# Attention, a token and channel mixer and a Fourier layer on one core: separate PSUM tiles for the banks of scores, transposes and the first stage, one exponential per block of queries, another table of the planner

## The chip, the cores and the metric

The kernel runs as one program on one core of a Trainium2 chip. The metric is the device time of an execution in microseconds (us). Before the change the median of 3 runs is 1688.03 us (1684.77 to 1692.13). One further execution was profiled; its own time is 1692.11 us.

TensorE (PE) multiplies matrices and writes only to PSUM, a memory of eight banks of 128 partitions by 512 words. VectorE (DVE) and ScalarE (ACT) read PSUM and write the results to SBUF, GpSimd (POOL) works in SBUF alone, and SyncE (SP) starts the DMAs. Each engine works off its own instructions in the order in which the program gives them, and waits at an instruction for semaphores that other engines raise.

## The reference

Attention over 4 batches of 8 heads, with 576 queries (neighbouring pairs of 1152 rows are averaged) and 1152 keys of 64 numbers; then two layers on the 4 x 576 x 512 result:

```python
q_pool = q.reshape(B, H, S // 2, 2, D).mean(axis=3)
scores = scale * np.matmul(q_pool, k.transpose(0, 1, 3, 2))
scores = scores - np.max(scores, axis=-1, keepdims=True)
attn = np.exp(scores)
attn = attn / (np.sum(attn, axis=-1, keepdims=True) + 1e-09)
x = np.matmul(attn, v)                               # heads side by side: 4 x 576 x 512

h = np.maximum(xt @ w_tok1, 0.0) @ w_tok2            # xt: tokens last; 576 -> 256 -> 576
u = x + h.transpose(0, 2, 1)
x = u + np.maximum(u @ w_ch1, 0.0) @ w_ch2           # 512 -> 1536 -> 512

u = x + np.real(np.fft.fft(np.fft.fft(x, axis=1), axis=2))
un = (u - mu) / np.sqrt(var + 1e-06)                 # over the 512 channels
out = u + np.maximum(un @ w_ch1, 0.0) @ w_ch2        # 512 -> 2048 -> 512
```

All of it is float32 with float64 weights for the mixers.

## The kernel before

Most products are made of several float32r products, of a number's rounded part ("hi") and its rest ("lo"): ACT copies a PSUM tile rounded, DVE subtracts that copy from the tile.

**Three stages.** (1) Heads 0 to 7 (`ALONE = 8`; functions `first_peaks`, `first_unit`) find the maxima first and make the scores with keys on the partitions. Their PSUM tiles are two pairs of banks (ring `pss_r`): PE writes the scores of two key blocks (line L742), ACT takes the exponential (L747), PE multiplies by the values (L754). (2) Heads 8 to 31 (`peaks`, `unit`, five blocks of 128 queries a head, the last of 66): PE writes a block's scores into three banks in six products of 384 columns (L637), DVE finds the row's maximum over the three banks (`nm<-m`, L644), ACT takes the exponential into SBUF with the sum beside it (`s<-m,nm`, L649) in two instructions, one over two banks and one over the third. Later PE turns `s` over, 128 x 128 at a time (L793), into a PSUM bank, ACT copies that rounded (`ph`, L797), DVE makes the rest (`pl`, L800), and PE multiplies both by the values into the tile `av` (L807). Beside these heads runs the mixer of the batch before (`mix`, L914 to L1038, weights converted from float64 on ACT, POOL and DVE in `slot`), whose products fill PE between the steps of attention. (3) The last batch's mixer, the Fourier layer (L1155, L1174) and the last channel mixer (L1442, L1501).

**PSUM.** One bank is `av`, three are the pool of `bank` tiles, which the mixer, the transposes and others share, and four are one tile, `m`:

```python
m_tile = ps_s.tile([128, 4, 512], F32, name="m", bufs=1)
pss_r = Ring(2, two, True)                                   # stage 1: m_tile[:, 0:2], m_tile[:, 2:4]
m3_r = Ring(3, lambda: m_tile[:, next(turn_3) % 3])          # stage 2: scores
t_bank = Ring(1, lambda: m_tile[:, 3])                       # stage 2: every second group of transposes
ps, ph, pl = Buf(t_bank if gr % 2 else banks), Buf(ph_r), Buf(pl_r)
```

So in stage 2 a head's groups of transposes go in turn to a `bank` tile and to the fourth bank of `m`; the trace shows them as `bank<-ident,s` and `m<-ident,s`.

**Order.** Nothing is ordered while the kernel runs. Every operation is given to a planner (`Plan`) with an engine, an estimated cost, a due time and its predecessors; the due time is shifted by a number from the table `SHIFT`. The planner runs a list schedule over the engines (`order`): whenever an engine is free, it takes the ready operation with the earliest due time whose ring has room. The order of taking is the order in which the program is written, and each engine keeps it. Semaphores are put in afterwards by the layer below, from the tiles that instructions read and write, and not from the planner's predecessors.

Of the kernel before, what the change touches and what calls it, by code (L numbers as in the profile page):

```python
# [10 lines left out]
F32 = mybir.dt.float32  # L11
# [20 lines left out]
PB = 5  # L32
# [29 lines left out]
    "cvld": 18.13, "cabs": 224.94, "cclamp": 670.62, "cshift": 760.61, "csign": 337.54, "cexp": 234.92, "cword":  # L62
    67.48, "cmul": 295.11, "cadd": 413.34, "chi": 147.28, "csub": 412.44, "cvst": 12.96, "cs": -377.28, "warm.":
    302.33, "l.": -504.19, "q.": -172.47, "qh.": 261.8, "ql.": -251.03, "kh.": 149.84, "kl.": 33.1, "M.":
    -589.13, "mr.": -66.27, "zh.": -31.41, "mr2.": -564.09, "zl.": -842.44, "mT.": 113.74, "mrow.": -729.51,
    "vld": -190.88, "S.": -511.53, "exp.": 571.95, "AV.": -220.28, "xe.": 223.11, "turn": -12.73, "rs": 1.74,
# [6 lines left out]
    "AV": -0.01, "xe": 0.2, "xa": -231.39, "open": -26.94, "sqrt": -563.36, "fcld": -177.35, "fchi": -19.77,  # L73
    "fclo": 939.3, "nyld": -271.24, "nyh": -694.66, "fld": 11.96, "FPUT": 293.06, "DFT": -6.81, "Zh": 398.17,
    "Zl": 102.01, "PB": -31.35, "PA": -31.32, "bs": -552.84, "pm": -30.79, "yadd": -115.75, "u2st": 433.32,
    "dwld": 8.26, "dwv": 9.66, "dwh": -444.21, "dwl": -424.67, "mixover": 120.41, "fnetover": -188.88, "uld":
    -353.69, "bn": 99.88, "bnr": -116.71, "un": -351.91, "dturn": -126.93, "dth": 21.37, "dtl": -264.84, "L":
    129.06, "drl": -119.51, "dll": -135.45, "dadd": 425.75, "dst": 485.52, "TB": -658.08, "TH": 528.64, "TL":
    -1176.01, "TA": 254.23, "WR": 157.96, "WH": -43.89, "WL": -140.73, "VR": -598.67, "LP": -688.42, "LE":
    1013.96, "LC": -997.5, "LH": -14.88, "LL": 318.59, "LQ": 872.8,  # L80
# [32 lines left out]
class Op:  # L113
    def __init__(self, key, eng, cost, due, emit, deps, after, new, uses):
        self.key = key
        self.moves = eng in ("SP", "AQ")
        eng = "A" if eng == "AQ" else eng
        self.eng, self.cost, self.due, self.emit, self.new, self.uses = eng, cost, due, emit, new, uses
# [10 lines left out]

def lag(a, b):  # L130
    if a == b:
        return 0.13 if a == "V" else 0.0
    return 0.26 if b == "T" else 0.2


class Plan:
# [14 lines left out]
    def order(self):  # L151
# [10 lines left out]
        while len(out) < len(self.ops):  # L162
# [8 lines left out]
            for eng, q in ready.items():  # L171
# [21 lines left out]
                busy = best.end  # L193
# [7 lines left out]
                heapq.heappush(wait, (best.end + 0.2, -1))  # L201
# [8 lines left out]
    def room(self, ring, now):  # L210
        return len(ring.live) < ring.n or all(u.end is not None and u.end + 0.2 <= now for u in ring.live[0].users)
# [9 lines left out]
def tile_attention_moe_fnet(  # L221
# [51 lines left out]
    with tc.manual_schedule():  # L273
# [12 lines left out]
        ps_s = pool("ps_s", space=PSUM, side="right")  # L286
# [22 lines left out]
        def t_dma(n):  # L309
            return n / 235e3  # L310
# [25 lines left out]
        def conv64(due, src, outs, parts, sums=None):  # L336
# [17 lines left out]
            a = add("cabs", "A", t_act(n), due, lambda: nc.scalar.activation(out=f32(hi()), in_=words(F32, 1), func=AF.Abs),  # L354
                    [o], uses=[w])
            a = add("cclamp", "P", t_pool(n), due, lambda: nc.gpsimd.tensor_scalar(  # L356
# [10 lines left out]
            o = add("cword", "A", t_act(n), due, lambda: nc.scalar.activation(  # L367
# [99 lines left out]
        def two():  # L467
            i = 2 * (next(turn_2) % 2)
            return m_tile[:, i:i + 2]
# [30 lines left out]
        def totals(i):  # L500
            t = sp.tile([128, 5, 2], F32, name=f"sum{i}", bufs=1)
# [14 lines left out]
        def first_pair():  # L516
            for g in range(2):
                x, kk, k2, qq = Buf(x_r[g]), Buf(kk_r), Buf(k2_r), Buf(qq_r)
                due = 30 * g - 40
                q_parts = ((0, 256), (256, NQ)) if g == 0 else ((0, NQ),)  # L520
# [58 lines left out]
        def pair(p):  # L579
# [3 lines left out]
            lq = add("lq", "SP", t_dma(128 * 8 * NQ), due, lambda: nc.sync.dma_start(  # L583
                out=f32(qx.t), in_=qT[b, h:h + 2].rearrange("h d t n -> (h d) t n")), new=[qx])
            lk = add("lk", "SP", t_dma(128 * 4 * S), due, lambda: nc.sync.dma_start(
# [3 lines left out]
            q = add("qs", "P", t_pool(NQ), due + 0.5, lambda: nc.gpsimd.tensor_scalar(  # L589
# [1104 lines left out]
```

## Time and profile before

| | |
|---|---|
| median of 3 runs | 1688.03 us |
| profiled execution | 1692.11 us, span 1690.3 us (first to last instruction) |
| PE busy | 1486.4 us, 88% of the span, 9019 products |
| DVE, ACT, POOL busy | 988.1 us (58%), 807.5 us (48%), 566.8 us (34%) |
| granted TensorE clock, mean | 0.95 of full |
| DMA | 270.37 MB, 160 GB/s mean |

A row of the page's costliest groups gives line, engine, operation, tile written, tile read, shape and count, then busy time and mean duration, then the time for which that engine sat idle just before these instructions and what ended it. In the page's slices PE is 7 to 9 tenths busy up to two thirds of the span and 9 tenths or more from there. The first score product of stage 2 starts at 189.0 us, the last transpose at 1135.6 us.

### The profile page before, as it was taken

The page shows a single profiled execution, that of the slowest core. Times are in us where ns is not written, and L with a number is a line of the kernel's source. Part 1 is how long each engine was busy: PE and PEld are TensorE (multiplying, and loading weights), DVE is VectorE, ACT ScalarE, POOL GpSimd, SP SyncE. Part 2 cuts the span into 40 slices and gives each one's busy share as a digit, 9 for nine tenths or more (in the row PEclk, how much of TensorE's full clock was granted, in tenths as well). Part 3 has the DMA queues.
Part 4 walks back from the last instruction along what each step waited for, and adds up shares of the span by engine and source line. Part 5 has one row for each costly group of instructions (what it writes and reads, how often), then busy time and mean ns, then how long its engine had stood idle before and what let it go on. Part 6 is the DMA issues. An engine that isn't in the chain of part 4 may idle for free.

```text
span 1690.3 us, 24731 instructions
## 1 busy us (share of the span) xinstructions
PE 1486.4 (88%) x9019; PEld 1320.4 (78%) x9019; DVE 988.1 (58%) x1854; ACT 807.5 (48%) x1774; POOL 566.8 (34%) x468
## 2 busy tenths in 40 slices
PE   8999887889787878878878877889999999999999
PEld 6677676778676767777757777788998988999997
DVE  7665555656665545566654656555766575647542
ACT  4445566555555555554555555444223354425331
POOL 4667844444354524254544444310111000000000
PEclk8999899988998879999998999989999999999999
DMA  5767665454555535455655454217762655454352
GB/s 144 208 176 199 205 175 148 138 174 122 169 160 161 157 94 158 132 161 162 187 150 160 139 176 140 90 60 228 240 188 73 220 187 174 159 203 162 141 185 93
DMA packets 112179, 270.37 MB, mean 160 GB/s; under 512 B 9971, under 2 KB 37748, under 8 KB 111767
## 3 DMA queue, kind: packets, MB, share of 16 engines
q1 hardware_dynamic: 112058, 268.79, 52.6%
q8 instruction: 71, 1.16, 0.3%
q14 instruction: 50, 0.41, 0.1%
HBM read 191.15 MB, written 44.86 MB: 140 GB/s over the span
## 4 chain that ended last, share of the span: by engine, by line
PE 51%; ACT 9%; DVE 8%; issue 3%; DMA 1%; POOL 0%; ACTq 0%; SPq 0%; DVEq 0%; POOLq 0%
PE bank L1442 8%; PE bank L999 7%; PE m L637 7%; PE y L1501 6%; ACT s L649 5%; DVE nm L644 5%; PE bank L979 4%; PE c L1501 4%; PE m L793 3%; ACT ph L797 3%; DVE pl L800 2%; PE bank L1312 2%; PE y L1334 2%; PE av L807 2%; PE c L1155 1%
## 5 line engine op out<-in xcount | busy, mean ns | idle before, releaser
L637 PE MATMUL m<-kk,qq 128*128 128x384 f32 (+1 forms) x720 | 188.8, 383 | 85.4 <-ACT s L649 61.0
L649 ACT ACTIVATE s<-m,nm 128x768 f32<-128x768 f32 (+1 forms) x240 | 177.0, 739 | 106.1 <-DVE pl L800 38.9
L644 DVE TENSOR_REDUCE nm<-m 128x1 f32<-128x1152 f32 (+1 forms) x120 | 162.5, 1354 | 98.6 <-PE m L793 40.5
L637 PEld LDWEIGHTS m<-kk,qq 128*128 128x128 f32 (+1 forms) x720 | 120.0, 192 | 126.0 <-ACT s L649 84.1
L979 PE MATMUL bank<-ut,w 128*128 128x320 f32 (+1 forms) x1152 | 190.6, 312 | 6.5 <-DVE pl L800 4.2
L800 DVE TENSOR_TENSOR pl<-m,ph 128x512 fp32r<-128x512 f32 (+1 forms) x144 | 80.1, 556 | 185.2 <-ACT s L649 70.1
L979 PEld LDWEIGHTS bank<-ut,w 128*128 128x128 f32 x1152 | 171.9, 202 | 8.9 <-issue 5.1
L999 PE MATMUL bank<-h,w 128*128 128x320 f32 (+1 forms) x1152 | 163.3, 298 | 1.6 <-DVE pl L800 1.0
L999 PEld LDWEIGHTS bank<-h,w 128*128 128x128 f32 x1152 | 157.6, 191 | 3.1 <-DVE pl L800 1.4
L1442 PE MATMUL bank<-tt,wc 128*128 128x320 f32 x1008 | 157.1, 309 | 1.2 <-DVE e L1456 1.1
L1442 PEld LDWEIGHTS bank<-tt,wc 128*128 128x128 f32 x1008 | 151.9, 188 | 6.6 <-DVE e L1456 1.3
L356 POOL TENSOR_SCALAR slot<-slot 128x512 f32<-128x512 f32 (+2 forms) x62 | 117.5, 1899 | 117.6 <-ACT slot L354 107.7
L797 ACT ACTIVATE ph<-m 128x512 fp32r<-128x512 f32 (+1 forms) x144 | 70.6, 490 | 176.0 <-DVE nm L644 78.6
L793 PE MATMUL m<-ident,s 128*128 128x128 f32 (+1 forms) x480 | 84.7, 296 | 72.3 <-ACT s L649 36.1
L807 PE MATMUL av<-ph,vv 128*128 128x256 f32 (+1 forms) x432 | 141.7, 343 | 2.0 <-DVE xtr L819 1.5
L369 POOL TENSOR_TENSOR slot<-slot 128x512 f32<-128x512 f32 (+2 forms) x62 | 81.3, 1312 | 175.9 <-DVE slot L364 151.5
L807 PE MATMUL av<-pl,vv 128*128 128x256 f32 (+1 forms) x432 | 129.5, 315 | 8.7 <-DVE pl L800 8.7
L793 PEld LDWEIGHTS m<-ident,s 128*128 128x128 f32 (+1 forms) x480 | 60.8, 155 | 94.5 <-ACT s L649 44.7
L797 ACT ACTIVATE ph<-bank 128x512 fp32r<-128x512 f32 (+1 forms) x192 | 88.8, 468 | 86.9 <-PE bank L793 84.7
L800 DVE TENSOR_TENSOR pl<-bank,ph 128x512 fp32r<-128x512 f32 (+1 forms) x192 | 99.1, 524 | 19.6 <-ACT ph L797 19.0
L1501 PE MATMUL y<-v,hp 128*128 128x512 f32 x432 | 108.2, 392 | 0.0
L1008 DVE TENSOR_TENSOR yt<-bank,yt 128x256 f32<-128x256 f32 (+1 forms) x192 | 85.4, 453 | 28.7 <-PE bank L999 26.2
(163 smaller groups left out, 2950.3 us busy)
## 6 DMA issues: line engine op xcount, KB each, us to landing
w<-wb_d SPq DMA_DIRECT2D x96, 512.0 KB
slot<-in_wm_dram SPq DMA_DIRECT2D x56, 512.0 KB
v<-w_d SPq DMA_DIRECT2D x24, 1024.0 KB
raw<-w_d SPq DMA_DIRECT2D x24, 896.0 KB
kk<-kx SPq DMA_DIRECT2D x66, 288.0 KB
wb_d<-slot SPq DMA_DIRECT2D x24, 512.0 KB
v<-in_v_dram SPq DMA_DIRECT2D x32, 292.5 KB
qx<-in_qT_dram SPq DMA_DIRECT2D x15, 576.0 KB
```

The source lines that it names most:

```text
L356: a = add("cclamp", "P", t_pool(n), due, lambda: nc.gpsimd.tensor_scalar(out=f32(hi()), in0=f32(hi()), scalar1=F64_LO, scalar2=F64_HI, op0 ...
L637: nc.tensor.matmul(m.t[:n, :KW], qq.t[:r, t, q0:q0 + n], kk.t[:r, c * KW:(c + 1) * KW], start=(t == 0), stop=(t == 1))
L644: a = add("mx" + own_place, "V", t_dve(S), d + 0.05, lambda n=n, j=j: nc.vector.tensor_reduce(out=nm.t[:n, j:j + 1], in_=m_tile[:n, :3, :K ...
L649: done.append(add("exp" + own_place, "A", t_act(KW * (c1 - c0)), d + 0.1, lambda s=s, n=n, j=j, k=k, c0=c0, c1=c1: nc.scalar.activation(ou ...
L793: nc.tensor.transpose(ps.t[:, at:at + r], made[j][0].t[:r, c * 128:(c + 1) * 128], ident[:r, :r])
L797: a = add("hi", "A", t_act(n), due + 0.1, lambda ps=ps, ph=ph, n=n: nc.scalar.activation(out=ph.t[:, :n], in_=ps.t[:, :n], func=AF.Copy), ...
L800: b = add("lo", "V", t_dve(n), due + 0.2, lambda ps=ps, ph=ph, pl=pl, n=n: nc.vector.tensor_tensor(out=pl.t[:, :n], in0=ps.t[:, :n], in1=f ...
L807: nc.tensor.matmul(po.t[:, :nq], vv.t[:, c].rearrange("p s d -> p (s d)"), x.t[:, k * nq:(k + 1) * nq], start=c == 0 and x is ph, stop=c = ...
L979: mms.append(lambda ps, k=len(mms), kk=kk, wi=wi, xi=xi, t0=t0, n=n: nc.tensor.matmul(ps[:, :n], view("p (s k n) -> p s k n", s=2, k=4)[:, ...
L999: mms.append(lambda ps, k=len(mms), x=x, wi=wi, hi=hi, cc=cc, t0=t0, n=n: nc.tensor.matmul(ps[:, :n], ww[x][2]("p (s n) -> p s n", s=2)[:, ...
L1442: nc.tensor.matmul(ps.t[:, :PH], w.t[:, wi, k, 128 * kk:128 * kk + 128], x.t[:, xi, kk], start=(first and m == 0), stop=(last and m == 5), ...
L1501: nc.tensor.matmul(y.t, h.t[:, k, hi, j * 128:(j + 1) * 128], v.t[:, wi, k], start=(q == 0 and k == 0 and n == 0), stop=(q == 7 and k == 1 ...
```

## The change

Four parts. (a) `m` is taken apart. Stage 1 has a pool of two tiles `s` of two banks. When the exponentials of head 7 are planned, that pool is closed, and in its place two tiles are opened: `m` of three banks for scores and `tr` of one bank for every second group of transposes. (b) The two exponentials of a block become one over 1152 columns, its sum is one number instead of two, and the DVE instruction that added the two goes. (c) The planner's costs change (hand-over times, an overlap of successive instructions on one engine, DMA rates, a least cost on DVE), and so do all numbers of `SHIFT`. (d) The operation that ends stage 1 waits for its exponentials alone.

```diff
 SHIFT = {
-    "cvld": 18.13, "cabs": 224.94, "cclamp": 670.62, "cshift": 760.61, "csign": 337.54, "cexp": 234.92, "cword":
+    "cvld": 76.82, "cabs": 1780.99, "cclamp": 658.29, "cshift": 534.18, "csign": 159.7, "cexp": 523.06, "cword":
...
+OVERLAP = {"A": 0.1, "V": 0.083, "P": 0.04}
+
+
 def lag(a, b):
-    if a == b:
-        return 0.13 if a == "V" else 0.0
-    return 0.26 if b == "T" else 0.2
+    if b == "T":
+        return 0.0 if a == "T" else 0.16 if a in OVERLAP else 0.26
+    if a == "T" or a not in OVERLAP or b not in OVERLAP:
+        return 0.2
+    if a == b == "A":
+        return -0.1
+    return 0.08 if b == "P" else 0.035
...
-                busy = best.end
+                busy = best.end - OVERLAP.get(eng, 0.0)
...
-            return n / 235e3
+            return n / 390e3
...
-        m_tile = ps_s.tile([128, 4, 512], F32, name="m", bufs=1)
-        turn_2 = iter(range(10 * ALONE))
+        m_tile = []
...
-        pss_r = Ring(2, two, True)
-        m3_r = Ring(3, lambda: m_tile[:, next(turn_3) % 3])
-        t_bank = Ring(1, lambda: m_tile[:, 3])
+        pss_r = Ring(2, lambda: early_s["s"].tile([128, 2, 512], F32, tag="s", name="s", bufs=2), True)
+        m3_r = Ring(3, lambda: m_tile[0][:, next(turn_3) % 3])
+        t_bank = Ring(1, lambda: m_tile[1])
...
-                done = []
-                for k, (c0, c1) in enumerate(((0, 2), (2, 3))):
-                    done.append(add("exp" + own_place, "A", t_act(KW * (c1 - c0)), d + 0.1, lambda s=s, n=n, j=j, k=k, c0=c0, c1=c1: nc.scalar.activation(
-                        out=s.t[:n, KW * c0:KW * c1].rearrange("p (c n) -> p c n", n=KW), in_=m_tile[:n, c0:c1, :KW], func=AF.Exp,
-                        bias=nm.t[:n, j:j + 1], accum_out=total.t[:n, j, k:k + 1]), [a],
...
+                o = add("exp" + own_place, "A", t_act(S) + 0.18, d + 0.1, lambda s=s, n=n, j=j: nc.scalar.activation(
+                    out=s.t[:n].rearrange("p (c n) -> p c n", n=KW), in_=m_tile[0][:n, :, :KW], func=AF.Exp,
+                    bias=nm.t[:n, j:j + 1], accum_out=total.t[:n, j]), [a],
+                    new=[s] + [total] * (j == 0), uses=ms + [nm] + [total] * (j > 0))
...
-                r = add("rs0", "V", 0.1, due - 0.5, lambda: nc.vector.tensor_reduce(
-                    out=rs.t, in_=total.t, axis=AX.X, op=ALU.add), [o for m in made for o in m[1]], new=[rs], uses=[total])
...
         def alone_over():
-            close(early_p["k2"])
+            close(early_p["k2"], early_s["s"])
             early_p["p"] = pool("p", side="right")
+            early_s["m"] = pool("ps_m", space=PSUM, side="right")
+            m_tile.append(early_s["m"].tile([128, 3, 512], F32, name="m", bufs=1))
+            m_tile.append(early_s["m"].tile([128, 512], F32, name="tr", bufs=1))
...
-                over = add("alone", "X", 0.1, 2 * ALONE, alone_over, last)
+                over = add("alone", "X", 0.1, 2 * ALONE, alone_over, m_free)
```

PE in stage 2, head 24, from its fourth block's scores to its fifth's, before:

```order
L637 MATMUL m<-kk_146,qq_148 128x384 x6
L793 MATMUL bank<-ident,s 128x128 x2
L793 MATMUL bank<-ident,s 128x66
L793 MATMUL m<-ident,s 128x128 x2
L793 MATMUL m<-ident,s 128x66
L793 MATMUL bank<-ident,s 128x128 x2
L793 MATMUL bank<-ident,s 128x66
L807 MATMUL av<-ph,vv 128x320
L807 MATMUL av<-pl,vv 128x320
```

The same place after the change (scores are L644 there, the mixer's second layer L1001, the product by the values L811, transposes L797):

```order
L644 MATMUL m<-kk_145,qq_147 128x384 x6
L1001 MATMUL bank<-h,w 128x256 x18
L811 MATMUL av<-ph,vv 128x256
L811 MATMUL av<-pl,vv 128x256
L811 MATMUL av<-ph,vv 128x256
L811 MATMUL av<-pl,vv 128x256
L1001 MATMUL bank<-h,w 128x256 x6
L1001 MATMUL bank<-h,w 128x320 x24
L843 MATMUL bank<-ident,xtr_132 128x65 x5
```

Between these two blocks stood three groups of transposes, one of them into `m`; now mixer products stand there, and the transposes have moved to other gaps.

ACT at the end of the same head, from the exponentials of its last block to those of the next block, before:

```order
L649 ACTIVATE s,sum_156<-m,nm 66x768
L649 ACTIVATE s,sum_156<-m,nm 66x384
L856 ACTIVATE x_5569<-xs 128x5x64
L797 ACTIVATE ph<-bank 128x320
L797 ACTIVATE ph<-m 128x320
L797 ACTIVATE ph<-bank 128x320
L649 ACTIVATE s,sum_158<-m,nm 128x768
L649 ACTIVATE s,sum_158<-m,nm 128x384
```

And after the change (exponentials L654, rounded copies L801, a copy of the mixer L902):

```order
L654 ACTIVATE s,sum_155<-m,nm 66x1152
L801 ACTIVATE ph<-bank 128x256
L902 ACTIVATE h<-bank 128x256
L801 ACTIVATE ph<-bank 128x320
L801 ACTIVATE ph<-tr 128x320
L801 ACTIVATE ph<-bank 128x320
L654 ACTIVATE s,sum_157<-m,nm 128x1152
```

Each pair of exponentials is one instruction, and the copy of a group of transposes between two blocks reads `tr` where it read `m`.

## Rows read from the trace of the kernel before

**Rows 1.** Windows: length, busy PE, PEld, DVE, ACT, POOL (instructions), granted clock, DMA

```profile
0.00:189.00 189.00, 172.86 (x857) 129.81 (x857) 119.81 (x245) 95.67 (x180) 121.67 (x98) 0.95 0.67 181
189.00:1136.00 947.00, 769.73 (x4861) 689.21 (x4862) 549.37 (x979) 510.40 (x1195) 417.06 (x331) 0.92 0.50 149
1136.00:1690.00 554.00, 543.79 (x3305) 501.35 (x3303) 318.96 (x631) 201.40 (x401) 28.06 (x39) 1.00 0.53 172
300.00:420.00 120.00, 100.91 (x621) 92.22 (x621) 71.34 (x134) 62.75 (x146) 55.70 (x39) 0.86 0.50 150
660.00:780.00 120.00, 96.48 (x661) 87.62 (x661) 70.03 (x129) 64.31 (x151) 51.10 (x43) 0.99 0.57 167
```

**Rows 2.** Waits of PE, longest first: us in total, times, longest

```profile
PE m L637 <- ACT s L649: 61.0, 76, 2.3
PE m L793 <- ACT s L649: 36.1, 35, 2.9
PE m L793 <- DVE nm L644: 32.6, 35, 1.5
PE m L637 <- ACT ph L797: 19.7, 34, 1.2
PE av L807 <- DVE pl L800: 8.7, 12, 1.6
PE m L742 <- ACT s L747: 4.9, 9, 1.3
```

**Rows 3.** Costliest groups of the page: scores, transposes and their copies, by tile

```profile
L637 PE MATMUL m<-kk,qq 128*128 128x384 f32 (+1 forms) x720 | 188.8, 383 | 85.4 <-ACT s L649 61.0
...
L800 DVE TENSOR_TENSOR pl<-m,ph 128x512 fp32r<-128x512 f32 (+1 forms) x144 | 80.1, 556 | 185.2 <-ACT s L649 70.1
...
L797 ACT ACTIVATE ph<-m 128x512 fp32r<-128x512 f32 (+1 forms) x144 | 70.6, 490 | 176.0 <-DVE nm L644 78.6
L793 PE MATMUL m<-ident,s 128*128 128x128 f32 (+1 forms) x480 | 84.7, 296 | 72.3 <-ACT s L649 36.1
...
L797 ACT ACTIVATE ph<-bank 128x512 fp32r<-128x512 f32 (+1 forms) x192 | 88.8, 468 | 86.9 <-PE bank L793 84.7
L800 DVE TENSOR_TENSOR pl<-bank,ph 128x512 fp32r<-128x512 f32 (+1 forms) x192 | 99.1, 524 | 19.6 <-ACT ph L797 19.0
```

**Rows 4.** PE's groups: the transposes into bank tiles

```profile
L793 PE MATMUL bank<-ident,s 128*128 128x128 f32 (+1 forms) x600 | 100.1, 287 | 0.9 <-ACT yo L1038 0.8
```

**Rows 5.** Waits in 189 to 1136 us: maxima (L644) and exponentials (L649)

```profile
DVE nm L644 <- PE m L793: 40.5, 31, 3.0
ACT s L649 <- DVE pl L800: 38.9, 61, 1.8
DVE nm L644 <- ACT ph L797: 21.1, 17, 3.7
ACT s L649 <- PE m L793: 19.9, 27, 2.5
ACT s L649 <- PE m L637: 19.6, 22, 1.9
```

**Rows 6.** Groups by shape: the maximum

```profile
L644 DVE TENSOR_REDUCE nm<-m 128x1 f32<-128x1152 f32 x96 | 130.0, 1354 | 77.5 <-PE m L793 30.1 <-PE m L637 29.0 <-ACT ph L797 14.0
```

**Rows 7.** Timeline of one block: start, us, instruction, idle time before it

```profile
703.86 0.90 ACT L649 ACTIVATE s<-m,nm 128x768 f32<-128x768 f32 x1
...
704.75 0.57 ACT L649 ACTIVATE s<-m,nm 128x384 f32<-128x384 f32 x1
705.22 0.20 ACT L649 ACTIVATION_READ_ACCUMULATOR s<-m,nm 128x1 f32 x1
...
705.47 0.50 PE L793 MATMUL m<-ident,s 128*128 128x128 f32 x3 [1.53 <-ACT s L649]
```

**Rows 8.** Chain that ended last, 1040 to 1052 us: start, us, what

```profile
1044.03 6.39 PE bank L999 x48
```

More of the change, by code (lines that the diff above doesn't have):

```diff
@@ L61 @@
 SHIFT = {
-    "cvld": 18.13, "cabs": 224.94, "cclamp": 670.62, "cshift": 760.61, "csign": 337.54, "cexp": 234.92, "cword":
[L63 to L66, printed above, removed]
[6 rows of a table removed]
@@ L73 @@
[L73 to L77, printed above, removed]
@@ new lines @@
+    596, "l.": -1129.82, "q.": -389.69, "qh.": 813, "ql.": 487.06, "kh.": 285.17, "kl.": 1348.93, "M.":
+    -1368.75, "mr.": 395.41, "zh.": -1263.97, "mr2.": -873.19, "zl.": -1496.10, "mT.": 553.72, "mrow.":
+    -1077.02, "vld": -30.01, "S.": 515.13, "exp.": 1066.74, "AV.": 182.42, "xe.": 354.06, "turn": -423.86, "rs":
[7 rows of a table added]
+    -1202.55, "sqrt": -1837.85, "fcld": -303.77, "fchi": 918.09, "fclo": 352.26, "nyld": -804.71, "nyh": 403.06,
+    "fld": 78.32, "FPUT": -325.75, "DFT": -35.78, "Zh": 720.42, "Zl": 1112.17, "PB": -31.07, "PA": -31.07, "bs":
@@ L81 @@
+    1040.85,
 }
@@ L117, in __init__ @@
         eng = "A" if eng == "AQ" else eng
-        self.eng, self.cost, self.due, self.emit, self.new, self.uses = eng, cost, due, emit, new, uses
+        self.eng, self.cost, self.due, self.emit, self.new, self.uses = eng, max(cost, 0.16) if eng == "V" else cost, due, emit, new, uses
         self.deps, self.after = deps, after
@@ L200, in order @@
                 heapq.heappush(wait, (busy, -1))
-                heapq.heappush(wait, (best.end + 0.2, -1))
+                heapq.heappush(wait, (best.end + (0.2 if best.moves else free_lag(eng)), -1))
                 out.append(best)
@@ L210, in room @@
     def room(self, ring, now):
-        return len(ring.live) < ring.n or all(u.end is not None and u.end + 0.2 <= now for u in ring.live[0].users)
+        return len(ring.live) < ring.n or all(u.end is not None and u.end + (0.2 if u.moves else free_lag(u.eng)) <= now for u in ring.live[0].users)
     def issue(self):
@@ L285, in tile_attention_moe_fnet @@
         ps_a = pool("ps_a", space=PSUM, side="right")
-        ps_s = pool("ps_s", space=PSUM, side="right")
+        early_s = {"s": pool("ps_s", space=PSUM, side="right")}
         ps_f = pool("ps_f", bufs=NB, space=PSUM)
@@ L500, in totals @@
         def totals(i):
-            t = sp.tile([128, 5, 2], F32, name=f"sum{i}", bufs=1)
+            t = sp.tile([128, 5, 1], F32, name=f"sum{i}", bufs=1)
             nc.vector.memset(t, 1.0)
@@ L639, in scores @@
                                 start=(t == 0), stop=(t == 1))
-                    parts.append(add("M" + own_place, "T", t_pe(2, KW), d, scores, q_op + k_ops[c] + [z] + (m_free if g == ALONE and j == 0 else []), m_last,
+                    parts.append(add("M" + own_place, "T", t_pe(2, KW), d, scores, q_op + k_ops[c] + [z] + ([over] if g == ALONE and j == 0 else []), m_last,
                                      new=[m], uses=[kk, qq]))
@@ L644, in peaks @@
                 a = add("mx" + own_place, "V", t_dve(S), d + 0.05, lambda n=n, j=j: nc.vector.tensor_reduce(
[L645 removed]
+                    out=nm.t[:n, j:j + 1], in_=m_tile[0][:n, :, :KW], axis=AX.XY, op=ALU.max, negate=True),
                     parts, new=[nm] * (j == 0), uses=ms + [nm] * (j > 0))
[L647 to L653 removed]
+                o = add("exp" + own_place, "A", t_act(S) + 0.18, d + 0.1, lambda s=s, n=n, j=j: nc.scalar.activation(
+                    out=s.t[:n].rearrange("p (c n) -> p c n", n=KW), in_=m_tile[0][:n, :, :KW], func=AF.Exp,
+                    bias=nm.t[:n, j:j + 1], accum_out=total.t[:n, j]), [a],
+                    new=[s] + [total] * (j == 0), uses=ms + [nm] + [total] * (j > 0))
+                made.append((s, [o]))
             ops[g] = made, total
@@ L748, in first_unit @@
                     out=ex(), in_=ps.t[:, :n, :HQ], func=AF.Exp), prev, new=[s], uses=[ps])
-                if i == 2 * ALONE - 1 and gr > 2:
-                    m_free.append(a)
+                m_free.append(a)
                 def av(c0=c0, n=n, ex=ex):
@@ L793, in turned @@
                             nc.tensor.transpose(ps.t[:, at:at + r], made[j][0].t[:r, c * 128:(c + 1) * 128], ident[:r, :r])
-                t = add("T" + own_place, "T", len(cs) * (0.222 if half == 0 else 0.285), due, turned, [o for j in blocks for o in made[j][1]] + (m_free if g == ALONE else []), in_turn["T"], new=[ps], uses=src)
+                t = add("T" + own_place, "T", len(cs) * (0.222 if half == 0 else 0.285), due, turned, [o for j in blocks for o in made[j][1]] + [over], in_turn["T"], new=[ps], uses=src)
                 in_turn["T"] = [t]
@@ L847, in head_out @@
                 made, total = ops[g]
-                r = add("rs0", "V", 0.1, due - 0.5, lambda: nc.vector.tensor_reduce(
-                    out=rs.t, in_=total.t, axis=AX.X, op=ALU.add), [o for m in made for o in m[1]], new=[rs], uses=[total])
                 r = add("rs0", "V", 0.08, due - 0.5, lambda: nc.vector.tensor_scalar(
-                    out=rs.t, in0=rs.t, scalar1=1e-9, scalar2=None, op0=ALU.add), [r], uses=[rs])
+                    out=rs.t, in0=total.t, scalar1=1e-9, scalar2=None, op0=ALU.add), [o for m in made for o in m[1]], new=[rs], uses=[total])
             r = add("rs1", "V", 0.08, due - 0.5 * (g >= ALONE), lambda: nc.vector.reciprocal(out=rs.t, in_=rs.t), [r], uses=[rs])
@@ L1533, in attention_over @@
         def attention_over():
-            close(ps_s, ps_a, early_p["p"], sp, kq)
+            close(early_s["m"], ps_a, early_p["p"], sp, kq)
             fr["raw"] = pool("wraw", side="right")
```

41 lines of the change are left out of this document (20 added, 21 removed), and 13 rows, old and new, of the table SHIFT.

## The prediction

> **What bounds the kernel now.** I read first the windows by stage [rows 1]. From 1136 us on PE is busy for 543.79 of 554 us at the full clock, and up to 189 us for 172.86 of 189. The stretch between, in which heads 8 to 31 run beside the mixers of three batches, has 947 us and only 769.73 of PE: 177.3 us of idle time, while DVE (549.37), ACT (510.40) and POOL (417.06) have less work still. No engine is full there, so what bounds it is a chain of waits. The list of PE's waits names it [rows 2]: nearly everything is a wait at an instruction that writes the tile `m`. By the page's groups [rows 3] PE idled 85.4 us before score products and 72.3 us before transposes into `m`, 157.7 us in all.
>
> The question is which of these waits the arithmetic needs. The trace has a control: groups of transposes go in turn to `m` and to a `bank` tile, from the same `s`, and their results meet the same two engines. Before those into a bank PE idled 0.9 us over 600 products [rows 4], before those into `m` 72.3 us over 480. ACT idled 86.9 us before 192 copies from a bank and 176.0 us before 144 from `m`; DVE 19.6 us and 185.2 us before the rests [rows 3]. What ended the waits says why: a transpose into the fourth bank waited for the maximum (32.6 us) and for the exponential (36.1 us) [rows 2], which touch banks one to three alone; the copy of the fourth bank for the maximum (78.6 us); and in the other direction the maximum for transposes and for their copies (40.5 and 21.1 us), the exponential for the rest `pl`, for transposes and for score products (38.9, 19.9 and 19.6 us) [rows 5]. Whatever touches the four-bank tile waits for whatever touched it before, whichever bank that was. Two streams that share no number run in single file through it.
>
> **The change part by part.** The profiled execution took 1692.11 us, 1.8 us of it outside the span, and lies 4.1 us above the median of the three runs; I sum against it and take 4 us off at the end.
>
> *Separate tiles, stage 2: what goes.* Transposes into `tr` no longer wait for scores' instructions: of 72.3 us I leave the 3.6 us that neither the exponential nor the maximum ended, so 68.7 us go. The 19.7 us of score products that waited for a copy of the fourth bank go. The 61.0 us in which they waited for the exponential before are needed in kind, since three banks hold one block. But that exponential was late: before it the maximum lost 40.5 + 21.1 = 61.6 us and the exponential itself 38.9 + 19.9 + 19.6 = 78.4 us to waits without need, 140.0 us over 120 blocks or 1.17 us a block, more than the mean wait of 61.0 / 76 = 0.80 us. I take all 61.0 us away and build up anew below what is late next. Gone: 149.4 us.
>
> *What is late next.* Score products wait for the maximum and the exponential of the block before. Bare, that chain is 1.35 us of maximum [rows 6], one exponential over 1152 columns, which I estimate from the two of 768 and 384 at 0.90 + (0.90 - 0.57) = 1.23 us, and 0.2 us for reading the sum [rows 7]: about 2.8 us. Against it stands what PE has to do between two blocks' scores. Counted in the changed order, with 133 ns for 320 columns [rows 8], other widths in proportion and 0.11 us for a transpose (three in 0.50 us [rows 7], of which the last 0.29 us [rows 4]), the median gap holds 3.3 us; against 2.8 us the 120 gaps lack 12 us in sum, against 3.3 us 28 us, against 4.0 us 84 us. The chain will be above bare, since the maximum stands in DVE's queue behind rests of about half a microsecond and the exponential in ACT's behind copies of about as much [rows 3]. I take 3.4 us and 34 us of new waits, bounds 12 and 84. Behind the waiting product stand transposes and products with values, which only PE delays. A PE that comes sooner also meets the rests `pl` sooner, for which it waits 8.7 us now [rows 2]: 12 us more, bounds 0 and 30. New waits: 46 us.
>
> *One exponential.* ACT's 0.90 + 0.57 us becomes about 1.23, and one read of the sum of two goes. On PE's path this is within the chain above, so it has no term of its own. The DVE instruction less per head and the instruction's place in DVE's queue I price at nothing: DVE idles for 40% of the stretch [rows 1]. Does the split do anything now? Score products waited mostly for the second exponential's end, not the first's: in the timeline PE sits idle from before the first and goes on at 705.47 us, after the second's sum at 705.42 [rows 7].
>
> The Trainium skill, page Perfetto Trace Analysis, section Optimizing Scalar/DVE Operations, speaks against this part: if ScalarE is not saturated but causes bubbles on other engines, breaking up its instructions may let work complete sooner. By it the joining would cost what a first part frees; that is a rival below.
>
> *The clock.* A mean of 0.92 over 947 us [rows 1] is, with the two levels 1.2 and 2.4 GHz, 2 x 0.08 x 947 = 152 us at the lower. At PE's busy share, 0.81, that is 123 us of work at half speed, 62 us dearer than at full. Where PE idles 2% the mean is 1.00, where 8.5% (to 189 us) 0.95, where 19% 0.92; but single windows do not follow (0.86 with 19.1 us of idle in 120, 0.99 with 23.5). With idle time down from 177 to 74 us I take half of it, 30 us back, bounds 0 and 62.
>
> The Trainium skill, page TensorE: Matmul & The Clock Gate, section A second HAM failure mode: psum-queue depth-cycling, says that a PE idling briefly between groups of products makes the clock go back and forth between its levels. By that rule all 62 us would come back, and the sum below would be 1520 us.
>
> *The rest.* Separate pairs in stage 1 touch its 4.9 us of waits [rows 2]: 3 us. The new order in the last 554 us has 10 us of PE idle time to play with: 0, bounds 5 either way. The work is the same 9019 products. Ending stage 1 costs one hand-over of PSUM, as now: 0.
>
> Sum: 1692.1 - 149.4 + 46 - 30 - 3 = 1555.7, less 4 for the median: about 1552 us. The likeliest case alone spans 1500 (new waits 25, all of the clock) to 1595 (new waits 70, 10 of the clock).
>
> **Rivals.** *The chain keeps the pace.* DVE and ACT are in-order queues with 0.5 us instructions before every maximum and exponential; with a real chain of 4 us or more PE's new waits are the upper bounds, 84 + 30, and the clock gives 10 us. For it: now the exponential is late in most blocks. Against it: 140 us of that lateness is without need. Time: 1692 - 149 + 114 - 10 - 3 - 4 = 1640.
>
> *The joined exponential holds the banks too long.* With a split one two banks would be free 1.23 + 0.2 - 0.90 = 0.53 us earlier, over 120 blocks 63 us at most; if every gap needs them, the gain falls by that: 1615. For it: score products waited for exponentials 76 times [rows 2]. Against it: the median gap's cover. This is what the Trainium skill's sentence on breaking up would have.
>
> *Slower.* The names that end PE's waits are only the last of several, and the waits are set by the queues' order, so that separate tiles free nothing; then the joined exponential still holds the first two banks 0.53 us longer in 120 blocks. That is 1692 + 63 - 4 = 1751. It decides if less than 63 of the 149 us are freed. Against it stands the control of the bank tiles.
>
> *It doesn't do what it says.* Waits go on as they are, because the new order puts other needed waits in the same places: 1680 to 1696.
>
> **How the numbers follow.** The forecast 0.70; the chain 0.14; the banks held too long 0.08; no effect 0.04; slower 0.04. Within 0.5% (8 us, about what a measurement of this kernel can tell) of 1688 lies only the fourth: faster 0.92, same 0.04, slower 0.04. The predicted time is the first case's, 1552. The range, 1500 to 1640, holds that case but for its edges, that of the banks and half of the chain's: about 0.82.
>
> **What would show it.** PE idle below 10 us before transposes into `tr` (L797), and about 35 us before scores (L644), ended by exponentials (L654) alone; 120 exponentials of 1.2 to 1.3 us; maxima (L651) ended by score products, hardly by transposes; DVE idle before rests from `tr` near that from banks; stage 2 in 790 to 830 us with PE busy for nine tenths and a granted clock of 0.95 or more. Wrong, if `tr` keeps tens of us of waits for maxima or exponentials, if the scores wait for more than 85 us, or if the clock stays at 0.92 with the gaps gone.

## The result and the profile after

The changed kernel takes 1483.66 us (median of 4 runs, 1476.44 to 1488.67) against 1690.08 us of the kernel before (4 runs, 1684.77 to 1692.51): a ratio of 0.878, interval 0.873 to 0.883. Forecast were 1552 us and a range down to 1500. The sign and the mechanism held, the gain was a half larger than said: 206 us, not the 136 that lie between the median of 1688 and the forecast.

The windows of the changed kernel's profile by the same three stages (length; busy PE, PEld, DVE, ACT and POOL with instructions; granted clock; DMA share, GB/s), to be laid beside [rows 1]:

```profile
0.00:191.40 191.40, 171.49 (x857) 134.16 (x857) 113.05 (x247) 96.89 (x183) 124.00 (x101) 0.93 0.66 179
191.40:906.40 715.00, 682.78 (x4868) 647.38 (x4869) 552.68 (x954) 461.01 (x953) 415.43 (x329) 0.98 0.66 197
906.40:1485.60 579.20, 553.75 (x3297) 503.21 (x3295) 316.23 (x630) 198.93 (x400) 29.50 (x39) 0.99 0.51 164
```

Stage 2 went from 947.0 to 715.0 us, 27 us more than the whole gain, and the last stage took 25 us of it back: from 554.0 to 579.2 us, with the same work. In stage 2 two numbers of PE changed and not one: idle time fell from 177.3 to 32.2 us, and its busy time for the same products from 769.73 to 682.78 us.

The longest waits of PE in the changed kernel (us in total, times, longest), for [rows 2]:

```profile
PE m L644 <- ACT s L654: 16.5, 18, 2.2
PE av L758 <- ACT xtr L762: 6.4, 3, 5.3
PE bank L1444 <- ACT e L1454: 4.8, 11, 1.4
PE s L747 <- ACT s L752: 4.6, 8, 1.7
PE tr L797 <- DVE pl L804: 4.5, 6, 2.2
...
PE av L811 <- DVE pl L804: 1.3, 4, 0.6
```

Transposes wait for no maximum and no exponential any more, scores for exponentials alone (16.5 of the 16.8 us before them). The groups that answer to [rows 3], [rows 4] and [rows 6] (busy us, mean ns | idle before, and what ended it):

```profile
L651 DVE TENSOR_REDUCE nm<-m 128x1 f32<-128x1152 f32 (+1 forms) x120 | 162.0, 1350 | 23.8 <-PE m L644 22.6
L644 PE MATMUL m<-kk,qq 128*128 128x384 f32 (+1 forms) x720 | 156.4, 350 | 16.8 <-ACT s L654 16.5
...
L654 ACT ACTIVATE s<-m,nm 128x1152 f32<-128x1152 f32 (+1 forms) x120 | 146.4, 1220 | 26.1 <-DVE nm L651 25.4
...
L804 DVE TENSOR_TENSOR pl<-bank,ph 128x512 fp32r<-128x512 f32 (+1 forms) x192 | 100.1, 523 | 24.0 <-ACT ph L801 23.6
...
L804 DVE TENSOR_TENSOR pl<-tr,ph 128x512 fp32r<-128x512 f32 (+1 forms) x144 | 79.2, 550 | 27.1 <-ACT ph L801 26.5
L797 PE MATMUL bank<-ident,s 128*128 128x128 f32 (+1 forms) x600 | 93.3, 268 | 1.7 <-ACT yo L1040 1.5
...
L797 PE MATMUL tr<-ident,s 128*128 128x128 f32 (+1 forms) x480 | 74.8, 271 | 4.5 <-DVE pl L804 4.5
```

DVE's idle time before the rests of the fourth bank fell from 185.2 to 27.1 us, close to the 24.0 us before those of the bank tiles, and PE's before its transposes from 72.3 to 4.5 us, close to 1.7: the two twins of the control are nearly alike now. The 720 score products take 156.4 us of PE where they took 188.8.

The timeline of one block in the changed kernel (start, us, instruction) shows what [rows 7] could not:

```profile
500.38 1.34 DVE L651 TENSOR_REDUCE nm<-m 128x1 f32<-128x1152 f32 x1
500.41 0.44 PE L797 MATMUL tr<-ident,s 128*128 128x128 f32 x3
...
501.00 0.43 ACT L801 ACTIVATE ph<-tr 128x320 fp32r<-128x320 f32 x1
...
501.97 1.22 ACT L654 ACTIVATE s<-m,nm 128x1152 f32<-128x1152 f32 x1
502.04 0.48 DVE L804 TENSOR_TENSOR pl<-tr,ph 128x320 fp32r<-128x320 f32 x1
```

Transposes are written to `tr` while the maximum reads `m`, and their rest is taken while the exponential reads `m`. Before, each of these pairs stood in single file.

### The profile page after: what moved, and what is told of

Its sections match the earlier page's. It is cut to its first block, busy times and chain, and to the rows that moved or that the text cites. A ratio compares the mean times of both kernels' runs of the same rounds, so it can differ in the third digit from the quotient of the medians.

```text
span 1485.6 us, 24381 instructions
## 1 busy us (share of the span) xinstructions
PE 1408.0 (95%) x9019; PEld 1284.7 (86%) x9019; DVE 982.0 (66%) x1830; ACT 756.8 (51%) x1534; POOL 568.9 (38%) x468
## 4 chain that ended last, share of the span: by engine, by line
PE 60%; DMA 17%; DVE 6%; ACT 6%; issue 5%; POOL 4%; SPq 1%; ACTq 0%; DVEq 0%; POOLq 0%
PE bank L1444 8%; PE bank L1001 7%; PE bank L981 6%; PE y L1503 6%; DMA slot<-in_wm_dram 6%; PE m L644 5%; PE av L811 4%; PE c L1503 3%; PE av L758 3%; PE bank L678 2%; PE bank L1314 2%; PE bank L797 2%; PE y L1336 2%; DMA w_d<-slot 2%; PE tr L797 2%
## 5 line engine op out<-in xcount | busy, mean ns | idle before, releaser
L981 PE MATMUL bank<-ut,w 128*128 128x320 f32 (+1 forms) x1152 | 177.0, 298 | 1.4 <-DVE pl L804 0.7
L651 DVE TENSOR_REDUCE nm<-m 128x1 f32<-128x1152 f32 (+1 forms) x120 | 162.0, 1350 | 23.8 <-PE m L644 22.6
L644 PE MATMUL m<-kk,qq 128*128 128x384 f32 (+1 forms) x720 | 156.4, 350 | 16.8 <-ACT s L654 16.5
L1444 PE MATMUL bank<-tt,wc 128*128 128x320 f32 x1008 | 159.6, 312 | 8.0 <-ACT e L1454 4.8
L1444 PEld LDWEIGHTS bank<-tt,wc 128*128 128x128 f32 x1008 | 150.1, 188 | 19.5 <-ACT e L1454 9.5
L981 PEld LDWEIGHTS bank<-ut,w 128*128 128x128 f32 x1152 | 159.9, 189 | 3.0 <-DVE pl L804 1.6
L1001 PE MATMUL bank<-h,w 128*128 128x320 f32 (+1 forms) x1152 | 160.6, 296 | 0.2
L654 ACT ACTIVATE s<-m,nm 128x1152 f32<-128x1152 f32 (+1 forms) x120 | 146.4, 1220 | 26.1 <-DVE nm L651 25.4
L1001 PEld LDWEIGHTS bank<-h,w 128*128 128x128 f32 x1152 | 156.3, 189 | 0.9 <-DVE h L905 0.5
L644 PEld LDWEIGHTS m<-kk,qq 128*128 128x128 f32 (+1 forms) x720 | 118.3, 182 | 27.7 <-ACT s L654 22.5
L801 ACT ACTIVATE ph<-bank 128x512 fp32r<-128x512 f32 (+1 forms) x192 | 90.1, 470 | 90.8 <-PE bank L797 89.8
L811 PE MATMUL av<-ph,vv 128*128 128x256 f32 (+1 forms) x432 | 130.8, 320 | 4.3 <-ACT ph L801 3.4
L811 PE MATMUL av<-pl,vv 128*128 128x256 f32 (+1 forms) x432 | 123.3, 303 | 1.9 <-DVE pl L804 1.3
L804 DVE TENSOR_TENSOR pl<-tr,ph 128x512 fp32r<-128x512 f32 (+1 forms) x144 | 79.2, 550 | 27.1 <-ACT ph L801 26.5
L797 PE MATMUL bank<-ident,s 128*128 128x128 f32 (+1 forms) x600 | 93.3, 268 | 1.7 <-ACT yo L1040 1.5
L1463 ACT ACTIVATE hp<-e 128x320 fp32r<-128x320 f32 x96 | 39.6, 462 | 106.0 <-PE y L1503 93.2
L1503 PEld LDWEIGHTS y<-v,hp 128*128 128x128 f32 x432 | 79.7, 188 | 15.0
```

The costliest lines, as they stand in the source:

```text
L644: nc.tensor.matmul(m.t[:n, :KW], qq.t[:r, t, q0:q0 + n], kk.t[:r, c * KW:(c + 1) * KW], start=(t == 0), stop=(t == 1))
L651: a = add("mx" + own_place, "V", t_dve(S), d + 0.05, lambda n=n, j=j: nc.vector.tensor_reduce(out=nm.t[:n, j:j + 1], in_=m_tile[0][:n, :, ...
L654: o = add("exp" + own_place, "A", t_act(S) + 0.18, d + 0.1, lambda s=s, n=n, j=j: nc.scalar.activation(out=s.t[:n].rearrange("p (c n) -> p ...
L797: nc.tensor.transpose(ps.t[:, at:at + r], made[j][0].t[:r, c * 128:(c + 1) * 128], ident[:r, :r])
L801: a = add("hi", "A", t_act(n), due + 0.1, lambda ps=ps, ph=ph, n=n: nc.scalar.activation(out=ph.t[:, :n], in_=ps.t[:, :n], func=AF.Copy), ...
L804: b = add("lo", "V", t_dve(n), due + 0.2, lambda ps=ps, ph=ph, pl=pl, n=n: nc.vector.tensor_tensor(out=pl.t[:, :n], in0=ps.t[:, :n], in1=f ...
```

## The experiments

They separate the parts of the change, which its diff mixes: the tiles, the exponential, the order. Ratios are to the kernel before in the same series of runs; in the series of the experiments it took 1691 to 1694 us.

| kernel | median, us | ratio (interval) |
|---|---|---|
| changed kernel | 1483.66 | 0.878 (0.873 to 0.883) |
| e1 order of before, separate tiles, two exponentials | 1463.03 | 0.864 (0.862 to 0.866) |
| e2 the same, one exponential in the second's place | 1465.09 | 0.866 (0.864 to 0.868) |
| e6 the same, one exponential in the first's place | 1429.71 | 0.844 (0.842 to 0.846) |
| e9 order of before, one tile, one exponential | 1644.25 | 0.973 (0.969 to 0.977) |
| e3 changed kernel, one tile in stage 2 | 1704.95 | 1.007 (1.004 to 1.011) |
| e7 changed kernel, two exponentials | 1490.61 | 0.880 (0.876 to 0.883) |
| e8 changed kernel, stage 1's pairs in one tile | 1482.87 | 0.875 (0.873 to 0.877) |
| e10 e6 with stage 1's pairs in one tile | 1439.59 | 0.850 (0.848 to 0.853) |
| e4 changed kernel, its last stage in the order of before | 1457.50 | 0.861 (0.859 to 0.864) |
| e5 the same, and stage 1 too | 1457.18 | 0.860 (0.856 to 0.864) |

**e1, the tiles alone.** The kernel before, its table and its two exponentials, with nothing but the tiles taken apart (the pair of stage 2 is opened at its first use):

```diff
-        m_tile = ps_s.tile([128, 4, 512], F32, name="m", bufs=1)
...
+        def stage_2():
+            if not m_tile:
+                close(early_s["s"])
+                early_s["m"] = pool("ps_m", space=PSUM, side="right")
+                m_tile.append(early_s["m"].tile([128, 3, 512], F32, name="m", bufs=1))
+                m_tile.append(early_s["m"].tile([128, 512], F32, name="tr", bufs=1))
+            return m_tile
...
-        t_bank = Ring(1, lambda: m_tile[:, 3])
+        t_bank = Ring(1, lambda: stage_2()[1])
```

> The kernel before with its own order and its two exponentials, only with separate PSUM tiles (two of two banks in stage 1; in stage 2 one of three banks for scores and one of one bank for every second group of transposes). Theory (the shared tile made the waits): PE's waits before transposes into the fourth bank fall from 72 us to under 10, before scores from 85 to about 40, time 1530 to 1580 us. Rival (the new order made the gain, the waits named are only the last of several): 1670 us or more, with the waits in other places.

It took 1463 us, 67 us less than the theory's lower end and 20 us less than the whole change; the waits came as expected. Its waits of PE and its window of stage 2:

```profile
PE m L641 <- ACT s L653: 36.1, 55, 2.3
...
PE tr L797 <- DVE pl L804: 1.6, 3, 0.8
```

```profile
176.90:905.60 728.70, 681.87 (x4861) 640.62 (x4862) 547.80 (x979) 497.79 (x1195) 419.41 (x332) 0.99 0.65 193
```

Not one instruction stands elsewhere than before, and all but 1.6 us of the transposes' waits is gone, with 218 us of the stage. The tiles do this by themselves.

**e3, the tiles undone in the changed kernel.**

```diff
-            m_tile.append(early_s["m"].tile([128, 3, 512], F32, name="m", bufs=1))
-            m_tile.append(early_s["m"].tile([128, 512], F32, name="tr", bufs=1))
+            four = early_s["m"].tile([128, 4, 512], F32, name="m", bufs=1)
+            m_tile.extend([four[:, :3], four[:, 3]])
```

> The changed kernel in its own order, but in stage 2 scores and transposes share one tile of four banks again; stage 1 stays apart. Theory (the shared tile made the waits): most of the gain goes, 1640 to 1720 us, PE waits before scores and before transposes into the fourth bank again over 120 us together, and the granted clock of stage 2 back to about 0.92. Rival (the order made the gain): under 1530 us.

All of the gain went, as the theory had it: 1705 us. PE's waits and the window of stage 2:

```profile
PE m L797 <- DVE nm L651: 43.0, 47, 1.4
PE m L797 <- ACT s L654: 31.7, 21, 2.7
PE m L644 <- DVE pl L804: 28.3, 39, 2.4
PE m L797 <- DVE pl L804: 24.4, 27, 2.0
PE m L644 <- ACT ph L801: 19.1, 38, 0.7
PE m L644 <- ACT s L654: 8.6, 10, 2.2
```

```profile
188.20:1130.90 942.70, 771.35 (x4868) 694.06 (x4869) 548.00 (x954) 472.79 (x953) 415.74 (x330) 0.91 0.50 149
```

The instructions are the same, in the same order; what differs is only whether two parts of PSUM are followed as one tile or as two. Four of the six waits are between parts that share no bank (the fourth and the last are not). With the waits the clock is back at 0.91 and PE's busy time at 771 us. The rival that the waits are set by the queues' order has fallen.

**e2, e6, e9 and e7: the exponential.** In e2, e6 and e9 the planner still plans two, so that the order stays, and one of them is not issued:

```diff
-                    ... lambda s=s, n=n, j=j, k=k, c0=c0, c1=c1: nc.scalar.activation(
-                        out=s.t[:n, KW * c0:KW * c1]..., in_=m_tile[0][:n, c0:c1, :KW], func=AF.Exp,
+                    ... lambda s=s, n=n, j=j, k=k: k or nc.scalar.activation(
+                        out=s.t[:n]..., in_=m_tile[0][:n, :, :KW], func=AF.Exp,
```

(e6; `k and` in e2; e9 has it in the kernel before with its one tile.) e7 issues two activations one behind the other where the changed kernel issues one.

> As the run before (separate tiles in the order of before), and one exponential per block in the place of the second of the two. Theory (only the chain gets shorter by the second start-up and the second reading of the sum, about 0.2 us, on the third of blocks that wait): 5 to 15 us less than with two. Rival (a joined exponential holds the first two banks 0.5 us longer): 10 to 60 us more than with two.

> Separate tiles in the order of before, with one exponential at the place of the first of the two. (In the earlier run of this kind it stood at the second's place, where in some blocks score products of the next block stood ahead of it, so that it read their scores.) Theory (ACT spends 0.2 us less per block and the scores' banks come free so much sooner): PE waits before scores fall from 36 us to about 25, time 5 to 12 us less than separate tiles with two exponentials, 1453 to 1458 us. Rival (joining holds the first two banks longer): 10 us or more above 1463.

> The kernel before in its own order, with its one tile of four banks for everything, and only the exponential joined (at the first one's place; the DVE instruction that adds two sums goes). Theory (through the shared tile everything waits for whatever came before, and the joined exponential only takes 0.2 us out of each block's file): 1660 to 1690 us, PE's waits before tile m still 130 us or more. Then the new order alone, this against the new order with one tile (1705 us), costs 15 to 45 us. Rival (joined, the first two banks are held longer): 1700 to 1755 us.

> The changed kernel in its own order with two exponentials (768 and 384 columns) in the place of each one of 1152, and two sums added by one more DVE instruction a head. Theory (a longer chain and nothing freed sooner, since scores wait for the last reader of their tile): 5 to 20 us slower than the changed kernel, PE waits before scores 25 to 45 us instead of 17. Rival (breaking up lets scores start sooner): 5 us or more faster.

e2 came out with e1, and I had built it badly: at the second's place the exponential comes later than the first one did, in some blocks behind first scores of the next block, so that it takes the exponentials of the wrong scores. So e2 isn't the kernel that was meant, and only e6 and e9 count for the exponential. e6 puts it at the first's place and wins 33 us over e1, about three times the upper end of what was expected; e9 wins 46 us over the kernel before (47 in its own series), so that the forecast of little or no gain was missed by 16 us and the rival, that joining costs, fell. Score products in e1 waited 36.1 us for exponentials (the row above). Those of e2, then e6:

```profile
PE m L641 <- ACT s L653: 47.5, 44, 2.1
```

```profile
PE m L641 <- ACT s L653: 12.9, 18, 2.1
```

In e9 the same wait is

```profile
PE m L637 <- ACT s L649: 13.8, 19, 2.0
```

where it was 61.0 us over 76 waits [rows 2]. Of the 36 us that stage 2 is shorter in e6 than in e1, 24 are idle time of PE (46.8 and 23.2 us) and 12 busy time. The next scores need the last exponential's end. In 31 of the 120 pairs of the kernel before, and of e1, another instruction stands between the two on ACT, and in e1 a pair takes 1.68 us from its start to its end in the mean, where one exponential takes 1.22. In the changed order (e7) two exponentials made the scores wait 23.2 us (28 times) in place of 16.5 (18 times), but the time of e7 can't be told from that of the changed kernel: the intervals overlap. There the effect of joining stays open.

**e4 and e5: the order.** e4 takes the changed kernel's planned order, but fills the places of everything from the last mixer on (2018 operations) with the sequence of the kernel before; e5 does so as well with the 896 operations ahead of the first score product of head 8.

```diff
-        for o in self.order():
+        for o in self.merged(self.order()):
```

> The changed kernel, but everything planned after the heads (the last mixer, the Fourier layer and the last channel mixer) keeps among itself the order that the kernel before gave it. After the last transpose the changed kernel takes 579 us where the one before took 554. Theory (the new order of this stage costs it): 560 us or less there, the whole 15 to 25 us faster than the changed kernel, about 1462 us. Rival (it is the earlier arrival, with weights or clock not ready): within 5 us of the changed kernel.

> The changed kernel with the order of before for all that stood ahead of the first score product of head 8 and for all that is planned after the heads; only heads 8 to 31 keep the new order. Theory (the new order gives back time at both ends: stage 1 took 177 us with separate tiles in the order of before, 191 in the new one; the last stage 555 against 579): about 1445 us, 12 us less than with the late order of before alone. Rival (stage 1's 14 us are not the order's): 1457 us.

The last window of e4 and the first of e5:

```profile
898.60:1453.90 555.30, 544.65 (x3297) 501.91 (x3295) 318.28 (x630) 200.71 (x400) 28.00 (x39) 1.00 0.52 171
```

```profile
0.00:175.80 175.80, 164.65 (x856) 129.41 (x856) 116.56 (x244) 95.88 (x180) 120.50 (x98) 0.97 0.72 194
```

The last stage is back at 555 us and e4 faster by 26 us, as the theory had it: the 25 us that the change lost there are the order's. In e5 the first stage fell by 10 us against e4's 185.6, but its scores then waited 27.5 us in 20 waits, up to 5.8 us each, and the middle went from 713.0 to 723.3 us: no gain over e4, expectation missed. The time is the one that the rival gave, but not for its reason, since stage 1 did become shorter. That the middle was planned for another beginning would explain the new waits; this isn't shown. One more edit stands in the changed kernel beside the four parts: the first pair's queries are split at 348 and not at 256. e5 has it too, so stage 1's 191 us don't come from it alone.

**e8 and e10: stage 1's pairs in one tile**, in the changed kernel and in e6:

```diff
-        pss_r = Ring(2, lambda: early_s["s"].tile([128, 2, 512], F32, tag="s", name="s", bufs=2), True)
+        four = early_s["s"].tile([128, 4, 512], F32, name="s", bufs=1)
...
+        pss_r = Ring(2, two, True)
```

> The changed kernel with its two pairs of stage 1 in one tile of four banks again; stage 2 stays apart. Theory (each pair's exponential and scores then wait for the other pair's, as they did before): stage 1 takes 8 to 14 us longer than 191 us, time about 1494 us. Rival (PE has other work in stage 1): no change, within 3 us.

> The best so far (separate tiles, one exponential, order of before; 1430 us), with the two pairs of stage 1 in one tile of four banks again. In the order of before stage 1 became 12 us shorter with separate pairs (189 to 177 us). Theory (the shared tile made that too): first score product of head 8 at 186 to 190 us, time about 1440. Rival (something else in the order of heads 8 on frees it, as sharing cost nothing in the new order): within 3 us of 1430.

In the changed order it makes no difference (1482.87 against 1483.66 us; here the rival was right), in the order of before it costs 9.9 us, as expected: the first score product comes at 188.2 us in e10, at 178.4 us in e6. So the new order hides what these tiles bring.

**The best version** is e6, the old order with the new tiles and the joined exponential, 1429.71 us, 54 us below the changed kernel. Its windows:

```profile
0.00:178.40 178.40, 166.37 (x856) 130.54 (x856) 116.48 (x245) 95.79 (x180) 120.80 (x98) 0.95 0.70 192
178.40:871.20 692.80, 669.59 (x4861) 638.84 (x4862) 538.61 (x955) 469.02 (x955) 420.63 (x332) 0.99 0.68 203
871.20:1426.60 555.40, 545.00 (x3304) 502.82 (x3302) 318.70 (x631) 201.52 (x401) 28.04 (x39) 1.00 0.52 172
```

Against the changed kernel it is 13 us shorter in stage 1, 22 in stage 2 and 24 in the last.

Laid out by parts, medians in us:

| | one tile | separate tiles | the tiles bring |
|---|---|---|---|
| order of before, two exponentials | 1690 | 1463 (e1) | 227 |
| order of before, one exponential | 1644 (e9) | 1430 (e6) | 214 |
| new order, two exponentials | not run | 1491 (e7) | |
| new order, one exponential | 1705 (e3) | 1484 | 221 |

The tiles bring 214 to 227 us in every row that can be filled, the joined exponential 33 to 46 in the old order (lines one and two), and the new order costs 54 to 61 (lines two and four). The medians come from several series, so a difference is good to some 4 us. The one tile of lines one and two serves stage 1 as well, that of e3 stage 2 alone; stage 1's pairs make 10 to 12 us of the first two differences.

## Why the prediction was half right

The cause was read rightly. What decided was the control in [rows 3] and [rows 4], two groups of transposes from the same source into different tiles; e1 and e3 show it from both sides. What failed is the sizes: three terms of stage 2 were 99 us too small together, one of them put at nothing because the products are the same, and two terms outside it were 31 us too favourable. That the errors stand against each other is luck; with stage 1 and the last stage as forecast the time would have been about 1455 us, further from 1552. In spans, 1690.3 to 1485.6 us:

| step of the prediction | predicted, us | measured, us |
|---|---|---|
| waits gone, less new waits, in stage 2 (-149.4 + 46) | -103.4 | -145.1 |
| clock | -30 | -56 |
| "The work is the same 9019 products": PE's busy time at the full clock, stage 2 | 0 | -31 |
| "Separate pairs in stage 1" | -3 | +2.4 |
| "The new order in the last 554 us" | 0 | +25.2 |

**"What is late next".** The 149.4 us did go. Of the 157.7 us before scores and transposes [rows 3] there are 16.8 + 4.5 = 21.3 left; with the sum's 34 us of new waits it would have been 42.3. The wait for rests before `av`, 8.7 us, was to grow by 12 and is 1.3 us: 19 us more. DVE's idle time before the rests of the fourth bank fell from 185.2 to 27.1 us, so they come sooner as well, which the sum had left out. These two make the difference of the first line, 41.7 us, nearly whole.

The mis-sized term is the 34 us, made from a chain of 3.4 us and gaps with a median of 3.3. The chain came out about as assumed: from the last score product's end the trace has a mean of 3.44 us to the exponential's end (5.24 before) and 3.53 to the end of reading its sum. But it comes to a wait in 18 blocks of 120 only. The gaps are longer than I had counted: PE is ready for the next scores 3.61 us after the last ones in the median, and a chain of 3.53 us in every block would lack 26.5 us. And I had put one mean chain against each gap. With each block's own chain the same sum is 15.6 us, near the 16.5 measured, since blocks with a long chain have a long gap: in the 39 with the longest chains PE has 4.73 us of work between the scores, in the other 80 it has 3.68. Why the two go together, as rests and copies are queued where transposes fill PE, I only argue.

**"The clock".** By the trace's record of the granted clock PE worked 139.2 us of its busy time at the lower of the two levels (1.2 and 2.4 GHz) in stage 2 before, and 27.2 us after; half of the difference, 56 us, is the gain. With the idle time gone most of it came back. The other kernels show the same, with 148.2 us at the lower level in e3 and 9.6 us in e6: where PE idles 18% of the stage the mean is 0.91, where 3% 0.99. The share of idle time alone doesn't set it: e9 has 0.95 at 18%. I halved the term on the ground of two windows of 120 us that did not follow [rows 1], which was too little to go by. The rule of the Trainium skill (page TensorE: Matmul & The Clock Gate, section A second HAM failure mode: psum-queue depth-cycling), by which short idling between groups makes the clock go back and forth, agrees with this trace: 0.92 became 0.98. By it I had given 62 us in a sentence apart, nearer than my own 30.

**"The work is the same 9019 products".** The work was the same, but not the time that it keeps PE busy. Take the half of the time at the lower clock from PE's busy time in stage 2: 769.73 - 69.6 = 700.1 us before, 682.78 - 13.6 = 669.2 after, for the same products. PE loses more by a stall than the stall. Over the kernels this goes with the number of gaps in stage 2 longer than 50 ns:

| | gaps | PE busy, less half of its time at the lower clock, us |
|---|---|---|
| before | 235 | 769.73 - 69.6 = 700.1 |
| e3 | 220 | 771.35 - 74.1 = 697.3 |
| e9 | 193 | 735.56 - 42.8 = 692.8 |
| e1 | 82 | 681.87 - 8.2 = 673.7 |
| e7 | 64 | 682.17 - 4.9 = 677.3 |
| after | 58 | 682.78 - 13.6 = 669.2 |
| e6 | 47 | 669.59 - 4.8 = 664.8 |

From the first to the last it is 35.3 us over 188 gaps, 0.19 us a gap. The others lie within 2.5 us of that line, and so do e4, e5, e8 and e10; e7 lies 9.3 us above it.

The single products show what it is. In an unbroken stream they overlap in the trace: 720 score products with a mean of 350 ns keep PE busy for 156.4 us (row above), not for 252. The first product behind a gap has nothing to overlap with. At the full clock it adds 0.24 us more than the same product adds in a stream (in e6, eight or more products behind a gap): 48.3 us for 205 such products before, 13.7 us for 56 after. The products behind the first one add no more than in a stream, less than 1 us in sum in either kernel. So nothing is slower behind a gap; one product's overlap is lost. In e7 another 65 products lose most of theirs without a gap of 50 ns before them, 12.3 us against 4.5 us in e6, which is most of its 9.3. So the 99 us that the sum lacked in stage 2 are 42 of waits, 26 of clock and 31 of this (34.6 by the single products).

**"The new order in the last 554 us ... 0, bounds 5".** This step failed. There were 10 us of idle time to win, but an order can also lose, which I did not look for. New waits of PE stand in that stage, such as 4.8 us for ACT at L1444 (row above), and its idle time went from 10.2 to 25.5 us by the windows. All four kernels with the new order there (after, e3, e7, e8) have 576 to 579 us, all others 554 to 557. In stage 1 the separate pairs are worth 10 us (e10 and e6), the order took them. What in the new table or the planner's costs does this isn't known: the parts of the order were put back by hand, the old table under the new costs wasn't tried.

**"One exponential ... no term of its own".** Wrong in the order of before, 33 us (e6 against e1) to 46 (e9). I took [rows 7] to show that the scores went on after the second exponential, and concluded that the split did nothing. But the row at 705.47 us is of transposes into the fourth bank (L793), which by the control waited for the exponential through the shared tile alone; it says nothing of the scores. The split did harm, by the second instruction's own 0.25 us and by what stands between in 31 blocks. One block of a timeline was too few. The sentence of the Trainium skill on breaking up (page Perfetto Trace Analysis, section Optimizing Scalar/DVE Operations) is not borne out in the order of before: ACT is busy for 510 of 947 us, and still joining was better, since PE wants the last part's end. The predicted duration held: 1.22 us measured, 1.23 estimated.

**The rivals.** The chain does not keep the pace: its waits are 16.5 + 1.3 us and not 114. That a joined exponential holds the banks too long has fallen in the order of before (e6 and e9); in the new order e7 leaves it open. Slower and no effect have fallen with e1.

## What to carry to other kernels

Where two streams share a tile that is followed as one, look for a twin of the same work on a tile of its own: a difference in idle time before the twins shows that the sharing costs something, though not how much (71 us before PE's twins here [rows 3, 4], against 214 to 227 us in time), and taking the tile apart is an edit that can be tried with no instruction moved. Price a stall on PE by three terms: its idle time, the time at the lower clock, and some 0.2 us of lost overlap for the first product behind each gap; here the last two made 87 of the 232 us won in stage 2. And measure a change of order by itself, since beside a large gain its loss of 54 us could not be seen.

## What the runs showed of the hardware that was not expected

PE's busy time is no measure of its work: in stage 2 the same 4861 to 4868 products were 669.59 to 771.35 us busy. Apart from the clock it is the first product behind a gap that makes the difference, by 0.24 us, while those behind it are as fast as in a stream. A single ACT exponential over 1152 columns of three banks (1220 ns) is 0.25 us shorter than one of 768 and one of 384 [rows 7], and its maximum beside it has not changed (1350 against 1354 ns [rows 6]).
